# Later chunks of a fused attention and MLP kernel: the denominator ahead of the outer product, small matrix tiles, transfers inside SBUF, a new order

## The chip, the cores and the metric

One Trainium2 chip, one of its cores. A core has a matrix engine (TensorE, PE in the profile, with its weight loads shown as PEld), a vector engine (VectorE, DVE), a scalar engine (ScalarE, ACT), GpSimd (POOL), and SyncE (SP), from whose queue this kernel issues every transfer. SBUF is the working memory of 128 partitions, PSUM the small memory of eight banks that PE writes. The metric is the device time of one launch in microseconds (us); lower is better.

## The reference

```python
# q, k, v: (4 batches, 4 heads, 1088 positions, 32); S1, S2: (8, 32)
def phi(x):                                   # 64 features of each position
    a = einsum('rd,bhsd->bhsr', S1, x)        # 8 numbers
    b = einsum('rd,bhsd->bhsr', S2, x)        # 8 numbers
    return outer(a, b).reshape(..., 64)
kv  = einsum('bhsf,bhsd->bhfd', phi(k), v)    # 64 x 32 for each batch and head
z   = sum(phi(k), over positions)             # 64
num = einsum('bhsf,bhfd->bhsd', phi(q), kv)
den = einsum('bhsf,bhf->bhs', phi(q), z) + 1e-6
x   = (num / den), heads side by side         # 4352 tokens x 128
h   = x @ w_in                                # 128 -> 2048
out = (h * clip(h + 3, 0, 6) / 6) @ w_out     # 2048 -> 128
```

q, k and v are 32-bit floats; S1, S2, w_in and w_out arrive as 64-bit floats and are turned into 32-bit numbers on the chip.

## The kernel before, in words

**Tiling.** The 4352 tokens are cut into nine chunks: chunks 0 to 7 of 512 tokens (two for each batch) and chunk 8 of 256 (the last 64 tokens of every batch). The 2048 hidden columns are cut into eight pairs of 128-column blocks; a *step* is one chunk with one pair, 72 in all. Tokens lie along the free dimension of `x`, so a step takes `x` (128 x 512) and gives `h` (two PSUM banks).

**One step.** PE forms `h` with three matmuls for each block: `x` is kept as a high and a low part (`xh`, `xl`), `w_in` likewise, and `xh*wi_hi + xh*wi_lo + xl*wi_hi` is summed (lines 812, 813, 818). ACT takes relu(h+3) into `g` (826), DVE makes `g = min(g, 6) * h` (829), ACT rounds it into `gh` (833), and POOL or DVE subtracts to get the rest `gl` (837). PE then adds `gh*wo_hi + gh*wo_lo` (858, 859) and `gl*wo_hi` (861) into `o`. These are 12 matmuls of 512 columns for a step, called the MLP matmuls below. After the last pair of a chunk, `o` is scaled and stored.

**Keys and values.** For each batch, nine tiles of 128 positions: PE makes the 16 numbers a, b of every head (`abps_k`, 531), ACT copies them (540), POOL or DVE forms the outer product `ph_k` (559), and PE sums `kvps` over the nine tiles (594), with a column of ones beside `v` so that z comes along. ACT copies the result into `kvb` (619).

**Queries.** Chunks 0 and 1 ("near", `NEAR = 2`) go through `queries`: `abps_q`, `ph_q`, PE transposes into `phps` (714), ACT copies to `phT`, PE multiplies by `kvb` into `nd` (637), which holds numerator and denominator; DVE adds 1e-6, inverts and divides into `x` (644 to 648), and PE transposes `x` into `xps` (665). Chunks 2 to 8 go through `far_queries`: two matmuls make `abps_q` with features along partitions (536), DVE transposes it in 32x32 blocks (544), POOL or DVE forms `ph_q`, DVE transposes again (`pht`, 746), and SP writes it to DRAM (`phd`, four transfers, 752) and reads it back as `phT` (757). After `nd` and the division the same is done for `x`: a DVE transpose (`xt`, 774), four transfers to DRAM (`xd`, 779) and one back (`xT`, 783). ACT and DVE or POOL then split `x` into `xh` and `xl` (682, 686).

**Weights.** Eight loads of 512 columns (`wiraw`, `woraw`); for each, ACT, DVE and POOL put the two 32-bit words together and round into high and low parts (400 to 421).

**Order.** Every engine runs its instructions in program order. That order is decided while the kernel is built: `Plan` collects the operations with an estimated cost, a due time and the buffers they need, and lists them. The due times come from `STEP`, `DUES`, `LEADS` and `SHIFTS`, the order of the first steps from `RAMP`, the first loads from `FIRST_LOADS`. An operation with two engines in its cost may go to either. Buffers are counted in `BUFS`; PSUM has two banks for `a`, four for `h` (two tiles of two), two for `o`.

## Time and profile before

| | |
|---|---|
| runs (us) | 243.3, 243.34, 244.62; median 243.34 |
| profiled execution | 244.0, of which the span from first to last instruction is 242.2 |
| granted PE clock | 1.00 throughout |
| PE busy | 231.9 us, 96% of the span |
| DVE, ACT, POOL busy | 178.0, 168.7, 135.7 us |
| transfers | 23.8 MB in 242 us |

A group row of the profile names the line, engine, operation, output and inputs, then count, total busy time and the mean of one instruction. A matmul's own duration includes its way through the array, and the next one starts before it ends; what counts for PE is the distance from start to start. A matmul of plain 32-bit numbers appears as two records. A row of the timeline gives start, duration and count of a run of like instructions. A row of waits gives the engine and line that waited, what it waited for, and the total, the number of times and the longest.

### The profile page before, as it was taken

To read this page: it belongs to the slowest core of one execution; us is meant where nothing else is said; L and a number is where in the kernel's file an instruction comes from. 1 tells how busy PE (TensorE), PEld (TensorE's weight loads), DVE (VectorE), ACT (ScalarE), POOL (GpSimd) and SP (SyncE) were. 2 spreads that over 40 slices of the span, in tenths; PEclk is the share of its full clock that TensorE was granted. 3 is DMA by queue.
4 is the path that set the end of the run, shared out by engine and by line. 5 is a ranking of instruction groups with operands and counts; after the bars stand their busy time and mean duration, and the time that the engine had idled before them with its cause. 6 is when DMAs were issued, how large, how long until landed. Compare 5 with 4: busy or idle time off the path is not lost.

```text
span 242.2 us, 5410 instructions
## 1 busy us (share of the span) xinstructions
PE 231.9 (96%) x2212; PEld 181.7 (75%) x2212; DVE 178.0 (73%) x223; ACT 168.7 (70%) x213; POOL 135.7 (56%) x88
## 2 busy tenths in 40 slices
PE   8599999998999989999999999999999999999994
PEld 3478777665777757788887888888888888888894
DVE  1597899999987977845675565865867987696771
ACT  3396998764387548678767956778558886777671
POOL 2599899978898704369443575606532130423240
PEclk9999999999999999999999999999999999999999
DMA  6999996666484532400001010000000010000101
GB/s 173 357 408 311 376 352 164 176 164 189 132 211 142 159 93 59 125 3 0 0 1 43 3 43 13 32 0 3 0 13 30 0 46 0 0 0 0 46 0 65
DMA packets 16471, 23.80 MB, mean 98 GB/s; under 512 B 1728, under 2 KB 9024, under 8 KB 16448
## 3 DMA queue, kind: packets, MB, share of 16 engines
q1 hardware_dynamic: 16448, 23.48, 30.0%
q8 instruction: 17, 0.28, 0.5%
q14 instruction: 6, 0.05, 0.1%
HBM read 16.26 MB, written 7.21 MB: 97 GB/s over the span
## 4 chain that ended last, share of the span: by engine, by line
PE 71%; DVE 11%; DMA 6%; ACT 3%; SPq 2%; POOL 2%; issue 2%; DVEq 0%; ACTq 0%
PE o L861 11%; PE h L812 11%; PE o L858 11%; PE o L859 11%; PE h L818 11%; PE h L813 11%; DVE g L829 4%; DMA xd<-xt 3%; DMA kT<-kT_dram 3%; PE nd L637 3%; ACT g L826 2%; DVE pht L746 2%; DVE ph_k L559 2%; SPq L779 1%; DVE ph_q L559 1%
## 5 line engine op out<-in xcount | busy, mean ns | idle before, releaser
L837 POOL TENSOR_TENSOR gl<-g,gh 128x1024 fp32r<-128x1024 f32 (+1 forms) x39 | 90.3, 2323 | 85.7 <-PE o L861 49.8
L829 DVE SCALAR_TENSOR_TENSOR g<-g,h 128x1024 f32<-128x1024 f32 (+1 forms) x72 | 82.5, 1158 | 39.5 <-ACT g L826 38.9
L826 ACT ACTIVATE g<-h 128x1024 f32<-128x1024 f32 (+1 forms) x72 | 69.3, 978 | 28.9 <-PE h L818 28.5
L833 ACT CAST gh<-g 128x1024 fp32r<-128x1024 f32 (+1 forms) x72 | 71.8, 1002 | 21.8 <-PE o L859 8.7
L812 PE MATMUL h<-xh,wi_hi 128*128 128x512 f32 (+1 forms) x148 | 57.2, 387 | 1.5 <-DVE g L829 1.5
L813 PE MATMUL h<-xh,wi_lo 128*128 128x512 f32 (+1 forms) x148 | 55.6, 376 | 0.0
L858 PE MATMUL o<-gh,wo_hi 128*128 128x512 f32 (+1 forms) x144 | 54.8, 383 | 0.0
L818 PE MATMUL h<-xl,wi_hi 128*128 128x512 f32 (+1 forms) x148 | 54.2, 379 | 0.6 <-DVE xl L686 0.6
L859 PE MATMUL o<-gh,wo_lo 128*128 128x512 f32 (+1 forms) x144 | 54.7, 382 | 0.0
L837 DVE TENSOR_TENSOR gl<-g,gh 128x1024 fp32r<-128x1024 f32 (+1 forms) x33 | 42.1, 1287 | 5.3 <-PE o L861 3.3
L861 PE MATMUL o<-gl,wo_hi 128*128 128x512 f32 (+1 forms) x144 | 43.1, 383 | 0.0
L812 PEld LDWEIGHTS h<-xh,wi_hi 128*128 128x128 f32 x148 | 27.7, 187 | 9.6 <-DVE g L829 3.2
L818 PEld LDWEIGHTS h<-xl,wi_hi 128*128 128x128 f32 x148 | 27.6, 188 | 7.1 <-DVE xl L686 1.5
L813 PEld LDWEIGHTS h<-xh,wi_lo 128*128 128x128 f32 x148 | 27.8, 188 | 5.2
L859 PEld LDWEIGHTS o<-gh,wo_lo 128*128 128x128 f32 x144 | 27.0, 188 | 5.7
L858 PEld LDWEIGHTS o<-gh,wo_hi 128*128 128x128 f32 x144 | 27.0, 187 | 5.7
L861 PEld LDWEIGHTS o<-gl,wo_hi 128*128 128x128 f32 x144 | 26.2, 188 | 5.7
L559 POOL TENSOR_TENSOR ph_q<-ab_q 128x512 f32<-128x512 f32 x12 | 13.2, 1105 | 2.8 <-DVE ab_q L544 2.8
L637 PEld LDWEIGHTS nd<-kvb,phT 128*32 128x32 f32 (+1 forms) x480 | 8.8, 113 | 4.2 <-issue 1.9
L637 PE MATMUL nd<-kvb,phT 128*32 128x66 f32 (+1 forms) x480 | 10.9, 223 | 0.7 <-issue 0.3
L594 PEld LDWEIGHTS kvps<-v,ph_k 128*32 128x32 f32 (+3 forms) x504 | 7.2, 113 | 2.7 <-issue 1.8
L559 POOL TENSOR_TENSOR ph_k<-ab_k 128x512 f32<-128x512 f32 (+1 forms) x7 | 7.0, 1012 | 3.5 <-ACT ab_k L540 2.3
(63 smaller groups left out, 164.6 us busy)
## 6 DMA issues: line engine op xcount, KB each, us to landing
phd<-pht SPq DMA_DIRECT2D x24, 128.0 KB, 2.5
phT<-phd SPq DMA_DIRECT2D x6, 512.0 KB, 3.8
qT<-qT_dram SPq DMA_DIRECT2D x8, 256.0 KB, 7.3
wiraw<-w_in_dram SPq DMA_DIRECT2D x4, 512.0 KB, 6.3
woraw<-w_out_dram SPq DMA_DIRECT2D x4, 512.0 KB, 7.8
outT_dram<-os SPq DMA_DIRECT2D x8, 256.0 KB, 2.0
xd<-xt SPq DMA_DIRECT2D x24, 64.0 KB, 2.0
xT<-xd SPq DMA_DIRECT2D x6, 256.0 KB, 2.7
```

Source lines behind the costliest of these rows:

```text
L559: engines[e].tensor_tensor(out, a_, b_, op=ALU.mult)
L637: nc.tensor.matmul(W["nd"][e : e + w, o : o + 2 * DV], T["phT"][:, p, i : i + w], kvb[batch_of(c0 + i)][:, p, :], start=True, stop=True)
L812: nc.tensor.matmul(T["h"][:, u, i:j_], wi_hi[:, f], x, start=True, stop=False)
L813: nc.tensor.matmul(T["h"][:, u, i:j_], wi_lo[:, f], x, start=False, stop=False)
L818: nc.tensor.matmul(T["h"][:, u, i:j_], wi_hi[:, f], x, start=False, stop=True)
L826: nc.scalar.activation(T["g"][:, :, :n], T["h"][:, :, :n], AF.Relu, bias=3.0, scale=1.0)
L829: nc.vector.scalar_tensor_tensor(T["g"][:, :, :n], T["g"][:, :, :n], 6.0, T["h"][:, :, :n], op0=ALU.min, op1=ALU.mult)
L833: nc.scalar.copy(T["gh"][:, :, :n], T["g"][:, :, :n])
L837: engines[e].tensor_tensor(T["gl"][:, :, :n], T["g"][:, :, :n], T["gh"][:, :, :n].bitcast(F32), op=ALU.subtract)
L858: nc.tensor.matmul(o, wo_hi[:, f], T["gh"][:, u, :n], start=first and u == 0, stop=False)
L859: nc.tensor.matmul(o, wo_lo[:, f], T["gh"][:, u, :n], start=False, stop=False)
L861: nc.tensor.matmul(o, wo_hi[:, f], T["gl"][:, u, :n], start=False, stop=last and u == 1)
```

## The change

1. Only chunk 0 is near (`NEAR = 1`). Chunks 1 to 8 take a new `far_queries`.
2. In it the denominator is taken before the outer product: with M = the sum over keys of a times b (8 x 8 for each head), den = b_q . (M^T a_q). A third set of 8 numbers for each query, (M^T S1) q, comes out of the same projection as a and b. POOL multiplies it with b, DVE sums and inverts, POOL divides a by it, and then the outer product is formed; `x` needs no division any more, and no separate numerator and denominator.
3. The projection (line 820 of the new kernel) is eight matmuls of 32 rows by 32 columns of the array for each chunk, the product with kv (868) eight matmuls of 64 by 32, each over 256 tokens. Both results lie in two PSUM banks, with the heads' places in the second bank exchanged. The second product gives `x` already with features along partitions: no transpose, no transfer for `x`.
4. `phT` is moved from SBUF to SBUF by eight transfers of 64 KB (862) in place of a write to DRAM and a read.
5. For every batch kv is accumulated transposed (632), M beside it (643); ACT copies both, PE transposes and multiplies (686, 689), ACT keeps `kvs` and the third set of projection columns (692, 693). Batch 0 does this beside its old `kvps`, which chunk 0 still uses.
6. The rest `gl` (now line 935) goes to POOL alone after the first six steps (`SHARED = 6`); `xl` goes to DVE alone; the outer products of the later chunks go to POOL alone.
7. Every load and store is one contiguous stretch of a DRAM array, which the host lays out.
8. All of the numbers that set the order are new (`RAMP`, `FIRST_LOADS`, `STEP`, `LEADS`, `SHIFTS` and the rest).

```diff
-NEAR = 2
+NEAR = 1
-BUFS = dict(..., x=2, ..., xturn=1, xT=2)
+BUFS = dict(..., x=1, ..., prod=1, kvt=2)
+SHARED = 6
...
+def stretch(t, i, j):
+    return t[i * P : j * P].rearrange("(p x) -> p x", p=P)
...
+        def kvt(_, t, i, T, vbox):
+            ps = place(i)
+            for h in range(H):
+                e = h * Q
+                nc.tensor.matmul(ps[e : e + Q, KVT : KVT + F], vbox[0][:, t, h * DV : h * DV + D],
+                    T["ph"][:, t, h * F : (h + 1) * F], ..., tile_position=(0, e))
+            e = i % 4 * Q
+            nc.tensor.matmul(ps[e : e + Q, KVT + F : KVT + F + Q], a_, b_, ..., tile_position=(0, e))
...
+        def fold(_):
+            nc.tensor.transpose(K["fps"][:, :DM], K["kvt"][:, : 2 * F], ident)
+            for h in range(H):
+                nc.tensor.matmul(K["fps"][e : e + Q, DM : DM + R], s_turn[:, e : e + Q], K["kvt"][:, ...], tile_position=(0, e))
+        def keep(_):
+            nc.scalar.copy(s_proj[:, b, C : C + R], K["fps"][:, DM : DM + R])
+            nc.scalar.copy(kvs[b], K["fps"][:, :DM])
...
-    def far_queries(c, due, psb, ndb, ph_eng):
+    def far_queries(c, due):
+        def proj(_):
+            for (r, b, i, j), h in product(spans, range(H)):
+                e, g = h * Q, (h ^ r) * Q
+                nc.tensor.matmul(T["ps"][r][g : g + Q, ...], s_proj[e : e + Q, b, :], qbox[0][e : e + Q, i:j], ..., tile_position=(e, g))
+        def cp(_, r):
+            nc.vector.transpose(T["ab"][:, r * half : (r + 1) * half], T["ps"][r][:, :half])
+        def prod(_):
+            nc.gpsimd.tensor_tensor(p[:, :, :R], v[:, :, 1, :], v[:, :, 2, :], op=ALU.mult)
+        def invert(_):
+            nc.vector.tensor_reduce(den, parts()[1], axis=mybir.AxisListType.X, op=ALU.add)
+            nc.vector.reciprocal(T["rden"], den)
+        def divide(_):
+            nc.gpsimd.tensor_tensor(v[:, :, 0, :], v[:, :, 0, :], T["rden"].broadcast_to(...), op=ALU.mult)
+        def outer(e, r): ...
+        def turn(_, r):
+            nc.vector.transpose(T["turn"][:, :, r * half : (r + 1) * half]..., src)
+        def move(_):
+            for g, f in product(range(4), range(2)):
+                e = (2 * (g % 2) + f) * Q
+                nc.sync.dma_start(T["phT"][e : e + Q, g // 2, :n], T["turn"][g * Q : (g + 1) * Q, f, :n])
+        def xmm(_):
+            for (r, b, i, j), h in product(spans, range(H)):
+                e, g = (h ^ r) % 2 * HP, h * Q
+                nc.tensor.matmul(T["xps"][r][g : g + Q, ...], kvs[b][e : e + HP, g : g + Q], T["phT"][e : e + HP, h // 2, i:j], ..., tile_position=(e, g))
...
-        o4 = plan.add({POOL: 2.35 * k, DVE: 0.07 + 1.067 * k}, ...)
+        o4 = plan.add({POOL: 2.35 * k, **({DVE: 0.07 + 1.067 * k} if n_step < SHARED else {})}, ...)
```

**Where instructions move: PE ahead of the first MLP matmul.** Names end in the chunk or batch and a buffer's number; `k2` is the first half of batch 1's keys. Before, the last rows ahead of `h_0_0` serve chunks 0 and 1:

```order
L637 MATMUL nd_0_0_369<-kvb0_136,phT_0_357 64x66 x8
L714 MATMUL phps_1_2_384<-ident_131,ph_q1_359 128x128 x4
L714 MATMUL phps_1_0_392<-ident_131,ph_q1_359 128x128 x4
L637 MATMUL nd_0_2_403<-kvb0_136,phT_0_357 64x66 x8
L637 MATMUL nd_1_2_422<-kvb0_136,phT_1_401 64x66 x8
L665 MATMUL xps_0_438<-ident_131,x_0_412 128x128 x2
L637 MATMUL nd_1_0_443<-kvb0_136,phT_1_401 64x66 x8
L665 MATMUL xps_0_438<-ident_131,x_0_412 128x128 x2
L812 MATMUL h_0_0_463<-xh_0_458,wi_hi_156 128x256
```

Now the same place holds chunk 0, batch 0's fold, two tiles of batch 1 and chunk 1's projection:

```order
L713 MATMUL nd_0_2_420<-kvb_133,phT_0_266 64x66 x8
L686 MATMUL kvs_0_447<-ident_128,kvt_0_415 128x128
L689 MATMUL kvs_0_447<-kvt_0_415,s_turn_139 32x8 x4
L740 MATMUL xps_0_455<-ident_128,x_0_431 128x128 x2
L632 MATMUL kvps_1_461<-ph_k2_438,v_2_208 32x64 x4
L643 MATMUL kvps_1_461<-ab_k2_429 32x32
L632 MATMUL kvps_1_461<-ph_k2_438,v_2_208 32x64 x4
L643 MATMUL kvps_1_461<-ab_k2_429 32x32
L740 MATMUL xps_0_455<-ident_128,x_0_431 128x128 x2
L820 MATMUL cps_1_0_484<-qT_1_212,s_proj_137 32x256 x4
L820 MATMUL cps_1_1_485<-qT_1_212,s_proj_137 32x256 x4
L910 MATMUL h_0_0_495<-xh_0_476,wi_hi_154 128x256
```

Chunk 1's transposes and its two `nd` are gone from there; the fold, kv of batch 1 and a projection have come in, and the projection, with the fold and its copies ahead of it, now stands before the first MLP matmul.

**PE in the middle of the program, one far chunk.** Before, chunk 5's product with `kvb`, between MLP matmuls:

```order
L861 MATMUL o_0_0_741<-gl_0_3_1383,wo_hi_158 128x512 x2
L637 MATMUL nd_5_0_1457<-kvb2_140,phT_5_1278 32x66 x16
L637 MATMUL nd_5_2_1476<-kvb2_140,phT_5_1278 32x66 x16
L812 MATMUL h_3_3_1427<-xh_3_1086,wi_hi_156 128x512
L813 MATMUL h_3_3_1427<-xh_3_1086,wi_lo_157 128x512
```

and now:

```order
L916 MATMUL h_4_0_1897<-xl_4_1599,wi_hi_154 128x512
L868 MATMUL xps_5_0_1919<-phT_5_1873,kvs2_142 32x256 x4
L868 MATMUL xps_5_1_1920<-phT_5_1873,kvs2_142 32x256 x4
L956 MATMUL o_2_4_1885<-gh_2_5_1755,wo_hi_156 128x512
L957 MATMUL o_2_4_1885<-gh_2_5_1755,wo_lo_157 128x512
```

Thirty-two matmuls of 66 columns have become eight of 256, and the place stands behind 384 MLP matmuls where it stood behind 133.

**POOL, at the last step of chunk 0.** Before:

```order
L837 TENSOR_TENSOR gl_1_3_1249<-g_1_3_986,gh_1_3_1223 128x1024
L559 TENSOR_TENSOR ph_q7_1290<-ab_q7_1244 128x512 x2
L837 TENSOR_TENSOR gl_1_5_1326<-g_1_5_1201,gh_1_5_1295 128x1024
L415 TENSOR_TENSOR w_wo2_1061<-w_wo2_1061,rest_wo2_1047 128x512
L837 TENSOR_TENSOR gl_0_3_1383<-g_0_3_665,gh_0_3_762 128x1024
```

and now, ahead of `gl_0_7`:

```order
L935 TENSOR_TENSOR gl_1_3_1270<-g_1_3_1157,gh_1_3_1203 128x1024
L935 TENSOR_TENSOR gl_1_7_1287<-g_1_7_1234,gh_1_7_1277 128x1024
L832 TENSOR_TENSOR prods_135<-ab_6_1272 128x16x8
L841 TENSOR_TENSOR ab_4_1174<-ab_4_1174,rden_4_1242 128x16x8
L850 TENSOR_TENSOR ph_4_1345<-ab_4_1174 128x512
L841 TENSOR_TENSOR ab_6_1272<-ab_6_1272,rden_6_1340 128x16x8
L850 TENSOR_TENSOR ph_6_1368<-ab_6_1272 128x512 x2
L832 TENSOR_TENSOR prods_135<-ab_8_1334 128x8x8
L850 TENSOR_TENSOR ph_4_1345<-ab_4_1174 128x512
L935 TENSOR_TENSOR gl_0_7_1410<-g_0_7_1268,gh_0_7_1343 128x1024
```

POOL now carries every `gl` of these steps but one, and small operations of three later chunks stand between two of them.

More of the change, by code (lines that the diff above doesn't have):

```diff
@@ L35 @@
 AB = 2 * H * R
+C = 2 * R
 CH = 512
@@ L271, in order @@
             for op in avail:
-                if op.ready > t or not all(b.held or any(free[g] for g in b.tags) for b in op.bufs):
+                if op.ready > t or not fits(op):
                     continue
@@ L636, in nd @@
                 i = (t + u) * P + e
[L637 removed]
+                nc.tensor.matmul(W["nd"][e : e + w, o : o + 2 * DV], T["phT"][:, p, i : i + w], kvb[:, p, :], start=True, stop=True)
         def norm(_):
@@ new lines, in far_queries @@
+        o1 = plan.add({PE: 0.1 + 0.43 * k}, due - LEAD["ab"], [lq, *done], proj, [qb, *pbs], 2 * n, recs=4 * H * len(spans), small=True)
+        cps = [plan.add({DVE: 0.12 + half / 960}, due - LEAD["cp"] + 0.3 * r, [o1], partial(cp, r=r), [pbs[r], abb]) for r in range(2)]
+        rdb = Buf(("rden",))
+        o2 = plan.add({POOL: 0.4}, due - LEAD["div"], cps, prod, [abb, prodb[0]])
+        o2 = plan.add({DVE: 0.45}, due - LEAD["div"] + 0.1, [o2], invert, [prodb[0], rdb])
+        o2 = plan.add({POOL: 0.4}, due - LEAD["div"] + 0.2, [o2], divide, [abb, rdb])
@@ new lines, in far_queries @@
+        prodb[0] = Buf(("prod",))
+        turned = []
+        for r in range(2):
+            cost = {POOL: 0.12 * blocks + 0.06}
+            o = plan.add(cost, due - LEAD["ph"] + 0.5 * r, [o2], partial(outer, r=r), [abb, phb])
+            turned.append(plan.add({DVE: 0.09 + blocks * F / 960}, due - LEAD["tr"] + 0.5 * r, [o], partial(turn, r=r), [phb, turnb]))
+        o = plan.add({SP: 8 * ISSUE}, due - LEAD["mv"], turned, move, [turnb, phTb], moved=n * 1.024, pieces=8)
+        o = plan.add({PE: 0.1 + 0.43 * k}, due - LEAD["nd"], [o, *done], xmm, [phTb, *xpbs, xhb], 2 * n, recs=4 * H * len(spans), small=True)
@@ L791, in fused_kernel, with step @@
+        split(c, due, [(lambda r=r: T["xps"][r], 0, r * half, (r + 1) * half, [o], xpbs[r]) for r in range(2)], xhb, LEAD)
     o_state = {}
-    def step(i, c, fp):
+    def step(n_step, c, fp):
         c0, n = CHUNKS[c]
-        due = when[i]
+        due = when[n_step]
         T = {}
```

347 lines of the change are left out of this document (192 added, 155 removed).

## The prediction

> **What bounds the kernel now.** I begin with the head of the page and then cut the span at the first MLP matmul and at the end of the interleaved work.
>
> ```profile
> span 242.2 us, 5410 instructions
> ...
> PE 231.9 (96%) x2212; PEld 181.7 (75%) x2212; DVE 178.0 (73%) x223; ACT 168.7 (70%) x213; POOL 135.7 (56%) x88
> ```
>
> ```profile
> 20.40:80.00 59.60, 57.49 (x1132) 42.72 (x1131) 54.98 (x93) 43.00 (x61) 54.74 (x37) 1.00 0.70 216
> 80.00:100.00 20.00, 18.79 (x166) 14.09 (x166) 16.57 (x21) 13.44 (x16) 5.91 (x3) 1.00 0.36 92
> 100.00:239.00 139.00, 138.97 (x644) 113.54 (x644) 94.73 (x87) 100.52 (x112) 61.62 (x28) 1.00 0.05 18
> ```
>
> The columns are the stretch, its length, then busy time and instructions of PE, weight loads, DVE, ACT and POOL, then the granted clock. From the first MLP matmul to 239 PE is idle for 2.1 + 1.2 + 0.0 = 3.3 us, at full clock throughout. The end is set by the amount of work on PE, by when it begins, and little else.
>
> ```profile
> 20.41 0.36 PE L812 MATMUL h<-xh,wi_hi 128*128 128x256 f32 x1
> ...
> 104.12 0.40 PE L812 MATMUL h<-xh,wi_hi 128*128 128x512 f32 x1
> ...
> 113.93 0.40 PE L858 MATMUL o<-gh,wo_hi 128*128 128x512 f32 x1
> ...
> 238.58 0.39 PE L861 MATMUL o<-gl,wo_hi 128*128 128x256 f32 x2
> 239.01 0.38 ACT L877 ACTIVATE os<-o 128x256 f32<-128x256 f32 x1 [2.40 <-PE o L861]
> ```
>
> Between 104.12 and 113.93 stand 42 starts of 512 columns, hence 9.81 / 42 = 0.2333 us each; 256 columns are taken as half, 0.1167.
>
> ```profile
> L858 PE MATMUL o<-gh,wo_hi 128*128 128x512 f32 x128 | 50.7, 396 | 0.0
> L812 PE MATMUL h<-xh,wi_hi 128*128 128x512 f32 x124 | 50.5, 407 | 1.5 <-DVE g L829 1.5
> ...
> L812 PE MATMUL h<-xh,wi_hi 128*128 128x256 f32 x24 | 6.7, 283 | 0.0
> ...
> L858 PE MATMUL o<-gh,wo_hi 128*128 128x256 f32 x16 | 4.1, 278 | 0.0
> ```
>
> Each count stands for three lines of the code, so there are 3 x (128 + 124) = 756 wide and 3 x (24 + 16) = 120 narrow MLP matmuls: 176.4 + 14.0 = **190.4 us**, which the change keeps. The budget of the span is then 20.4 (start) + 190.4 + 3.3 (waits) + 3.4 (last matmul near 238.8 to the end) and, as the rest, 24.7 us of small work on PE. That rest can be checked:
>
> ```profile
> L637 PE MATMUL nd<-kvb,phT 128*32 128x66 f32 x416 | 8.4, 223 | 0.7 <-issue 0.3 <-DVE x L648 0.3
> ...
> L594 PE MATMUL kvps<-v,ph_k 128*32 128x33 f32 x384 | 5.1, 198 | 0.2 <-issue 0.2
> ...
> L531 PE MATMUL abps_k<-s_ab,kT 128*32 128x64 f32 x216 | 4.1, 221 | 0.3 <-DVE w_wi L411 0.3
> L536 PE MATMUL abps_q<-qT,s_sb 128*64 128x256 f32 x24 | 3.7, 400 | 0.0
> ...
> L665 PE MATMUL xps<-ident,x 128*128 128x128 f32 x10 | 2.1, 295 | 0.0
> ...
> L594 PE MATMUL kvps<-v,ph_k 64*32 64x33 f32 x48 | 1.0, 197 | 0.0
> ```
>
> ```profile
> 73.93 1.14 PE L637 MATMUL nd<-kvb,phT 128*32 128x66 f32 x64
> 75.00 0.50 PE L812 MATMUL h<-xh,wi_hi 128*128 128x512 f32 x1
> 75.34 0.39 PE L813 MATMUL h<-xh,wi_lo 128*128 128x512 f32 x1
> ```
>
> After a visit to small work the first MLP matmul takes 75.34 - 75.00 = 0.34, which is 0.11 more than the pace; 17 visits make 1.9. With `nd` 8.4, `kvps` 6.1, keys 3.5 (184 of the 216 records come after 20.4), queries 3.4 (one of the calls comes early, chunk 8's is narrower) and transposes 1.3 (6 of 10), the sum is 24.6. It closes to 0.1.
>
> **The change, term by term: small work on PE.** What goes is `nd`, `abps_q`, the rest of `xps` and `kvps` in its old form: 8.4 + 3.4 + 1.3 + 6.1 = 19.2. What comes is priced from these two rows:
>
> ```profile
> 29.20 0.65 PE L536 MATMUL abps_q<-qT,s_sb 128*64 128x256 f32 x4
> ...
> 45.41 1.08 PE L536 MATMUL abps_q<-qT,s_sb 128*64 128x256 f32 x8
> ```
>
> Two more matmuls (four records), side by side in halves of the array, add 0.43; that is the length of one pass of 256 columns in plain 32-bit numbers. A projection is eight such matmuls on eight different tiles. If all run beside each other it costs 0.43 and the staggered starts of 16 records, at 1.07 / 64 = 0.017 each 0.27: 0.70. Bounds are 0.43 (nothing but the pass) and 8 x 0.43 = 3.4 (one after another). I take 0.70, near the 0.65 of the row of four. In favour of side by side: the `nd` row above ran 32 matmuls of 66 columns in 1.07; alone, each would need 66/256 of 0.43, 0.11, and 32 of them 3.5, so four column tiles did overlap fully. No row shows small tiles that overlap along the rows of the array.
>
> The Trainium skill ("TensorE: Matmul & The Clock Gate", Part 3, measured speedup) gives one pass and about 4 ns for each further tile, checked on sixteen tiles of 32 x 32; by that a product would cost some 0.46, and the forecast, as an estimate from that page, would lie about 3 us lower. The row's 0.65 for four records does not agree with so small a stagger, so I stay with 0.70.
>
> - Projections after the start, chunks 2 to 8: 6 x 0.70 + 0.5 = 4.7.
> - Products with kv, chunks 1 to 8: 7 x 0.70 + 0.5 = 5.4.
> - kv tiles: 36 in all, 11 of them ahead of the first MLP matmul. A tile has ten records (four of 64 columns and one of 32, two records each); at the keys' 4.1 / 216 = 0.019, 25 tiles are 4.75. Bounds: 0.012 as for `kvps` (5.1 / 384 = 0.013), 3.2; or 0.03, if switching tile shapes costs, 7.5.
> - Keys unchanged, 3.5.
> - Folds for three batches: a transpose at 2.1 / 10 = 0.21 and eight records, with ACT's copy between, 0.5 each, 1.5 (0.3 to 0.8 each).
> - Visits: 23 in the new order, 2.5.
>
> The sum is 22.35 against 24.6: **-2.2 us**.
>
> **The start.** Chunk 1's old query path goes from ahead of the first MLP matmul:
>
> ```profile
> 9.33 0.80 PE L531 MATMUL abps_k<-s_ab,kT 128*64 128x64 f32 x20 [2.35 <-DMA kT<-kT_dram]
> ...
> 13.90 0.69 PE L531 MATMUL abps_q<-s_ab,qT 128*64 128x64 f32 x16
> ...
> 17.12 1.09 PE L714 MATMUL phps<-ident,ph_q 128*128 128x128 f32 x8
> ...
> 19.60 0.69 PE L637 MATMUL nd<-kvb,phT 128*64 128x66 f32 x16
> ```
>
> That is 0.65 + 1.0 + 1.2 (two such `nd` rows) = 2.85. In come 11 kv tiles (nine of batch 0, which keeps its old `kvps` too, and two of batch 1), 110 records at 0.016 in a dense run, 1.75, a fold 0.4 and a projection 0.65: 2.8. The wait for the second part of the keys stays, since the same 1.34 MB go ahead of it. So 20.4 stands. From below: if ACT, which no longer copies chunk 1's `phT`, was late there, 19; from above: switches of tile shape and the small copies between, 22.
>
> **The waits.** DVE gives up 27 of its 28 wide `gl` and POOL takes them, and the wait at line 829 below is for DVE behind such work.
>
> ```profile
> PE h L812 <- DVE g L829: 1.5, 2, 1.2
> ```
>
> ```profile
> L837 POOL TENSOR_TENSOR gl<-g,gh 128x1024 fp32r<-128x1024 f32 x36 | 86.4, 2408 | 77.4 <-PE o L861 44.2 <-ACT gh L833 27.1 <-ACT g L826 6.0
> ...
> L837 DVE TENSOR_TENSOR gl<-g,gh 128x1024 fp32r<-128x1024 f32 x28 | 37.9, 1364 | 5.1 <-PE o L861 3.3 <-ACT gh L833 1.6
> ...
> L559 POOL TENSOR_TENSOR ph_q<-ab_q 128x512 f32<-128x512 f32 x12 | 13.2, 1105 | 2.8 <-DVE ab_q L544 2.8
> ...
> L415 POOL TENSOR_TENSOR w_wi<-w_wi,rest_wi 128x512 int32<-128x512 int32 x4 | 5.1, 1281 | 0.0
> L837 POOL TENSOR_TENSOR gl<-g,gh 128x512 fp32r<-128x512 f32 x3 | 3.8, 1292 | 8.3 <-PE o L861 5.7 <-ACT gh L833 2.7
> ...
> L464 POOL TENSOR_TENSOR s_ab<-s_parts 128x64 int32<-128x64 int32 x1 | 0.3, 318 | 1.3 <-DVE s_parts L459 1.3
> ```
>
> DVE falls from 178 to about 138. POOL rises to 63 x 2.41 + 8 x 1.29 + some 22 outer products at 1.1 + 19 of weights + 16 small ones = about 209 of 239. The small ones (`prod`, `divide`, 128 numbers a row) have no row; between 0.1 (the work share of a 512-number row, a quarter of 1.1 being 0.28, less if cheap) and 1.1, I take 0.33, beside the 0.32 of a 64-number row. What matters is the densest part, up to `gl_0_7` in the new order: 14 `gl` (33.7) + 16 outer products (17.6) + 15 weight operations (19.2) + 11 small ones (3.6) = 74.1 us. POOL starts these near 8.8, so it would be through at 82.9 without any wait. PE comes there after 200 MLP matmuls (46.7) and 17.8 of small work from 20.4, at 84.9. The slack is 2 us; POOL waited 59.6 - 54.74 = 4.9 us in that stretch before, with less of its own to do. So a little of it will show on PE: I take waits of 2.5 in place of 3.3, **-0.8**, with bounds 0.5 and 6.
>
> **Transfers.**
>
> ```profile
> phd<-pht SPq DMA_DIRECT2D x24, 128.0 KB, 2.5
> phT<-phd SPq DMA_DIRECT2D x6, 512.0 KB, 3.8
> ...
> xd<-xt SPq DMA_DIRECT2D x24, 64.0 KB, 2.0
> ```
>
> ```profile
> 239.42 0.33 SPq L880 DMA_DIRECT2D outT_dram<-os  x1
> ```
>
> Before, a far chunk waits 2.5 + 3.8 after its last transpose; now eight pieces of 64 KB at 2.0, issued 0.33 to 0.5 apart on SP, about 5 us; the path of `x` (2.0 and more) goes altogether. Between `move` and the product of a chunk stand at least two other steps of PE (5.6 us), the tightest for chunk 1, by hand with 1.7 us to spare. So nothing is booked; without that cover the cost is what lies over, up to 3 us once, which the range holds. Contiguous loads have no visible customer: after the start no wait of PE on a load is left to remove. SP is in order too: a `move` that waits for a turn holds up the stores and weight loads behind it, whose users come several steps later.
>
> **Sum.** 20.4 + 190.4 + 22.4 + 2.5 + 3.4 = 239.1 of span. The profiled execution took 244.0 with 242.2 of span; the median of the runs, 243.34, lies 1.1 above that span, so I add 1.1: **240.2 us**.
>
> **Rivals.**
>
> *The tiles overlap only four at a time* (0.07). Against it speaks nothing measured here; for it, that no row shows row tiles overlapping, and the four column tiles of `nd` are the most that ran at once. Each product then has a second pass of 0.43: 13 full and two half ones after the start 6.0, one in it 0.4: 246.6, slower than before. It decides from the first projection on: 0.70 or 1.13.
>
> *Tiles along the rows that write one bank run one after another* (0.04). Each bank of a projection takes four matmuls from four row tiles, 8 x 0.43 = 3.4 a projection (+2.7); a product with kv has two row tiles, 4 x 0.43 (+1.0). 7.5 x 2.7 + 7.5 x 1.0 = 28: 268. The overlap of the column tiles says nothing on it. The Trainium skill ("TensorEngine Tiling (Array Packing)", Restrictions and Gotchas, Gotcha 1) says that different row tiles cannot access the same PSUM bank at once, and would give this rival; the measured sixteen tiles of its other page speak against a strict reading, and no run here shows either yet.
>
> *POOL becomes the bound up to `gl_0_7`* (0.12). Beyond the 2 us of slack every wait of POOL is one of PE. If POOL waits as it did before, 4.9, and its small operations cost 0.5, PE waits 2.9 + 1.9 more: 245. For it: the 74.1 against 76.1. Against: operations stand in the order in which they come due, and 33 `gl` no longer compete for DVE.
>
> *The start does not hold* (0.12): switches between the 32-column and 128-column shapes and the copies of the fold in ACT's queue put the first MLP matmul at 22: 242.
>
> *Better than the sum* (0.10): start at 19, waits 0.5, small work at the lower bounds: 236.8.
>
> **How the numbers follow.** The forecast case has 0.55, with 238.2 to 242.2 of its own (0.5 for the kv tiles, 1 for the waits, 1 for the start). A measurement of this kernel can tell about 1% from no change, so faster means below 240.9 and slower above 245.8. Faster: 0.37 of the forecast and 0.10 of the better case, 0.47. Same: 0.18 of the forecast, 0.12 of the start, 0.07 of POOL, 0.37. Slower: 0.05 of POOL, 0.11 of the tiles, 0.16. The range runs from 236.5 to 246.6; the serial tiles and the ends of the other cases are left out.
>
> **What would show it.** Right: a projection and a product near 0.70 from start to next MLP matmul; first MLP matmul at 20 to 21; the kv tiles 0.19 each; PE idle after it below 3 us; POOL near 209 busy, DVE near 138; span near 239. Wrong: products of 1.1 or 1.7 to 3.4 (tiles); waits of PE on `gl` in the stretch to 85 (POOL); waits on `phT` (transfers); a first MLP matmul beyond 22.

## The result and the profile after

The changed kernel takes 247.27 us (median of 245.63, 246.08, 248.46 and 248.53) against 243.39 for the kernel before: ratio 1.0116 with an interval of 1.0069 to 1.0162, so slower by about 1.2%. Forecast were 240.2 and a range of 236.5 to 246.6. Further runs of the same kernel on another chip gave 247.25 (ratio 1.0114, 1.0068 to 1.0160). Here and below, times are medians of all runs and ratios leave out runs in the slower state, among them one of 319.6 us at a granted clock of 0.66 (the variant with the arrays as before).

The head of the page after, then the same cuts of the span as before (length; busy time and instructions of PE, weight loads, DVE, ACT, POOL; granted clock; share of the DMA engines; GB/s):

```profile
span 243.8 us, 4939 instructions
...
PE 232.0 (95%) x1958; PEld 176.6 (72%) x1959; DVE 132.6 (54%) x184; ACT 169.4 (69%) x228; POOL 210.2 (86%) x136
```

```profile
20.40:80.00 59.60, 57.29 (x783) 41.86 (x783) 46.47 (x73) 45.93 (x70) 56.84 (x41) 1.00 0.32 96
80.00:100.00 20.00, 18.32 (x129) 12.44 (x128) 12.73 (x24) 10.09 (x14) 17.79 (x16) 1.00 0.36 92
100.00:239.00 139.00, 138.17 (x701) 110.41 (x699) 63.14 (x67) 100.75 (x116) 122.06 (x60) 1.00 0.07 22
```

POOL's 210 and DVE's 133 are as forecast (209, 138), and the transfers of the stretch to 80 us fell to less than half (0.70 to 0.32). PE's idle time did not fall: 1.7 us in the middle stretch where there were 1.2, 0.8 in the last where there was none. The timeline gives the two ends:

```profile
22.09 0.39 PE L910 MATMUL h<-xh,wi_hi 128*128 128x256 f32 x1
...
239.50 0.50 PE L959 MATMUL o<-gl,wo_hi 128*128 128x256 f32 x2 [0.25 <-POOL gl L935]
240.03 0.38 ACT L975 ACTIVATE os<-o 128x256 f32<-128x256 f32 x1 [2.63 <-PE o L959]
```

The first MLP matmul comes 1.7 us later than before, the end of PE 1.0 later. PE's waits name the places (line, what was waited for, then total, number of times and longest):

```profile
PE o L956 <- ACT gh L931: 1.7, 1, 1.7
PE cps L820 <- issue: 1.4, 1, 1.4
PE abps_k L571 <- issue: 1.3, 1, 1.3
PE o L956 <- ACT kvt L682: 1.2, 1, 1.2
...
PE xps L868 <- DMA phT<-turn: 0.7, 1, 0.7
```

"Issue" is time in which an engine waits for nothing that the profile shows. Both cases lie ahead of the first MLP matmul and, as the timeline shows, in the middle of a run of like matmuls whose data were there already: after 4 of 32 records of the keys of batch 1, and after 13 of 16 of chunk 1's projection.

```profile
13.79 0.31 PE L571 MATMUL abps_k<-s_all,kT 128*32 128x64 f32 x4
15.40 0.58 PE L571 MATMUL abps_k<-s_all,kT 128*32 128x64 f32 x26 [1.31 <-issue]
...
19.52 0.65 PE L820 MATMUL cps<-qT,s_proj 32*32 32x256 f32 x13
21.54 0.62 PE L820 MATMUL cps<-qT,s_proj 32*32 32x256 f32 x3 [1.37 <-issue]
```

The row of `phT` shows less than was lost. A product with kv mostly takes 0.59 us from its start to the next MLP matmul. Two took longer (chunk 7's near 118, chunk 5's near 137), because the eight pieces of `phT` land one after another and each group of its matmuls waits for its own piece:

```profile
117.19 1.09 PE L868 MATMUL xps<-phT,kvs 64*32 64x256 f32 x6
118.99 0.64 PE L868 MATMUL xps<-phT,kvs 64*32 64x256 f32 x10 [0.70 <-DMA phT<-turn]
119.56 0.73 PE L959 MATMUL o<-gl,wo_hi 128*128 128x512 f32 x2
...
137.01 1.40 PE L868 MATMUL xps<-phT,kvs 64*32 64x256 f32 x16
138.35 0.50 PE L956 MATMUL o<-gh,wo_hi 128*128 128x512 f32 x1
```

The last pieces landed at 118.85 and 137.64. The two products took 2.37 and 1.34 us, together 2.5 more than twice 0.59, and the row counts 0.7 of that.

The budget of the span, with small work counted from start to start:

| us | forecast | measured |
|---|---|---|
| first MLP matmul | 20.4 | 22.1 |
| MLP matmuls | 190.4 | 190.4 |
| small work and visits | 22.4 | 23.6 |
| waits of PE after the start | 2.5 | 3.9 |
| last matmul to the end | 3.4 | 3.8 |
| span | 239.1 | 243.8 |

Of the 23.6, 1.8 is that uncounted part of the wait for `phT`. With it on the other side, small work is 21.8 and the waits are 5.7.

### The profile page after: what moved, and what is told of

It reads as the page before. It is cut to its first block, busy times and chain, and to the rows that moved or that the text cites. A ratio compares the mean times of both kernels' runs of the same rounds, so it can differ in the third digit from the quotient of the medians.

```text
span 243.8 us, 4939 instructions
## 1 busy us (share of the span) xinstructions
PE 232.0 (95%) x1958; PEld 176.6 (72%) x1959; DVE 132.6 (54%) x184; ACT 169.4 (69%) x228; POOL 210.2 (86%) x136
## 3 DMA queue, kind: packets, MB, share of 16 engines
q1 hardware_dynamic: 9264, 17.46, 22.1%
## 4 chain that ended last, share of the span: by engine, by line
PE 77%; POOL 11%; DMA 3%; issue 3%; SPq 3%; ACT 1%; POOLq 1%; DVE 1%
PE h L910 12%; PE o L959 12%; PE o L956 11%; PE h L911 11%; PE o L957 11%; PE h L916 11%; POOL gl L935 6%; POOL ph L850 3%; PE kvps L632 2%; DMA kT<-kT_dram 2%; SPq L862 2%; PE abps_k L571 2%; PE xps L868 1%; PE cps L820 1%; PE kvps L617 1%
## 5 line engine op out<-in xcount | busy, mean ns | idle before, releaser
L935 POOL TENSOR_TENSOR gl<-g,gh 128x1024 fp32r<-128x1024 f32 (+1 forms) x71 | 161.5, 2297 | 19.7 <-ACT gh L931 10.0
L931 ACT CAST gh<-g 128x1024 fp32r<-128x1024 f32 (+1 forms) x72 | 72.3, 1005 | 23.6 <-DVE g L927 8.6
L959 PE MATMUL o<-gl,wo_hi 128*128 128x512 f32 (+1 forms) x144 | 44.0, 387 | 0.2 <-POOL gl L935 0.2
L850 POOL TENSOR_TENSOR ph<-ab 128x512 f32<-128x512 f32 (+1 forms) x16 | 16.0, 1016 | 0.6
L856 DVE STREAM_TRANSPOSE turn<-ph 128x512 f32<-128x512 f32 (+1 forms) x16 | 10.2, 659 | 1.1 <-POOL ph L850 1.1
L760 DVE TENSOR_TENSOR xl<-xps,xh 128x256 fp32r<-128x256 f32 (+1 forms) x18 | 6.6, 401 | 5.4 <-ACT xh L756 4.5
L756 ACT CAST xh<-xps 128x256 fp32r<-128x256 f32 (+1 forms) x18 | 5.7, 366 | 5.3 <-PE xps L868 4.0
L825 DVE STREAM_TRANSPOSE ab<-cps 128x256 f32<-128x256 f32 (+1 forms) x16 | 6.5, 415 | 4.9 <-PE cps L820 4.5
L584 DVE TENSOR_TENSOR ph_k<-abps_k,ab_k 128x512 f32<-128x512 f32 (+1 forms) x15 | 8.4, 610 | 0.0
```

Source lines behind the costliest of these rows:

```text
L850: engines[e].tensor_tensor(out, a_, b_, op=ALU.mult)
L856: nc.vector.transpose(T["turn"][:, :, r * half : (r + 1) * half].rearrange("p f (t w) -> p t f w", w=Q), src)
L931: nc.scalar.copy(T["gh"][:, :, :n], T["g"][:, :, :n])
L935: engines[e].tensor_tensor(T["gl"][:, :, :n], T["g"][:, :, :n], T["gh"][:, :, :n].bitcast(F32), op=ALU.subtract)
L959: nc.tensor.matmul(o, wo_hi[:, f], T["gl"][:, u, :n], start=False, stop=last and u == 1)
```

## The experiments

The theory after the result: **PE's instructions arrive too late.** The page has this row for the transfers that carry instructions:

```profile
q8 instruction: 15, 0.25, 0.5%
```

That is 16.4 KB each, and PE's 1958 + 1959 instructions make 15.3 blocks of 256. Each record of a matmul has its weight load beside it, so a block is about 126 records, and the idle times of 1.31, 1.37 and 1.17 (the row that names `kvt`) stand right ahead of records 220, 346 and 599, one and two blocks apart. With all of PE's instructions in the trace counted, 449, 705 and 1217 come before them: 256 and 512 apart. ACT, which the third row names, had ended `kvt` at 32.14, 0.9 us before PE went on. The trace's instruction transfers, in us:

```
block boundary (record)     PE there   transfer begins, lands   PE goes on
changed, 220                10.0       12.86   13.88            15.40
changed, 346                15.4       19.12   20.17            21.54
changed, 599                28.3       30.72   31.67            33.05
before,  219                11.8       15.27   16.30            17.72 (no stall)
```

("PE there" is PE at the boundary before, when the block can be asked for.) A block takes 4.7 to 6.1 us from there until PE can use it: 2.4 to 3.7 before its transfer begins (the share of the DMA engines was 1.04, 1.03 and 0.69 in these stretches of the changed kernel), 1.0 to move, 1.4 to 1.5 more. PE used up the blocks ahead of the three stalls in 3.6 to 4.8 us; 126 MLP matmuls take 126 x 0.2333 = 29. The rivals: a data wait that the profile cannot name, or simply more work ahead of the first MLP matmul.

**The changed kernel again.**

> The changed kernel without an edit, to see which of its numbers come back. Its four runs fell into two pairs, 245.6 and 246.1 us at a mean granted clock of 0.997, and 248.5 twice at 0.986. Theory clock: the upper pair is the same schedule with about 5 us of half clock somewhere (1.1% of 240 us is 2.6 us, the distance of the pairs); then every run near 248.5 shows 0.985 to 0.987, and a profile of one shows a stretch of lower clock ahead of the last 4 us. Theory schedule: the upper pair has other waits of PE; then a profile near 248.5 shows them at full clock. Both expect the two idle times marked issue on PE near 14 and near 20, of 1.3 us each, the one of 1.7 before line 956 near 86, and the first MLP matmul at 22.1.

245.91 at a mean granted clock of 0.998, then 247.26, 247.63 and 247.24 at 0.991, 1.000 and 0.991. The idle times near 20 and 86 returned (1.46, 1.81). The one near 14 returned with the same length, but four records earlier and with another reason:

```profile
15.56 0.82 PE L571 MATMUL abps_k<-s_all,kT 128*32 128x64 f32 x30 [1.37 <-DMA kT<-kT_dram]
```

Here the load of batch 1's first keys landed at 15.43, where it landed at 13.65 in the first profile. The instruction block landed at 14.23; with the 1.4 to 1.5 from above it could be used near 15.7. So at this place PE goes on at the later of two arrivals, and taking away the instruction stall alone would have gained next to nothing in this execution. In the variants below these keys landed between 13.4 and 16.1. The idle time of 1.17 near 32 was 0.31 here, all of it ACT's, which ended `kvt` at 32.53.

The level of the time is not only clock: the run at 1.000 took 247.6. No run near 248.5 came back, so the two theories on the pairs stay open. But stretches at half clock do occur, as the next runs show.

**Warm-up matmuls cut into eight.**

```diff
-        nc.tensor.matmul(warm, ones[:, :P], ones, start=True, stop=True)
+        for i in range(8): nc.tensor.matmul(warm[:HP, : CH // 8], ones[:, :HP], ones[:, : CH // 8], start=True, stop=True)
```

> Each of the thirteen warm-up matmuls of 512 columns is cut into eight of 64, so that PE's program has some 182 more instructions ahead of its real work and hardly more to do. Theory instruction fetch: PE's program comes in blocks of 256 instructions (126 records of the profile), a block is asked for when the one before it is begun and takes 5 to 6 us while the loads run; the idle times stand at the records 220, 346 and 599, multiples of that block apart. Then they leave their old instructions (the fifth record of the keys of batch 1, the fourteenth of chunk 1's projection), stand some 91 records earlier in the program, where the block before them took longer to run, and sum to 0.5 us or so instead of 2.7 ahead of the first MLP matmul, which comes at 19.5 to 20.5; time 1.5 to 2.5 us below that of the changed kernel. Theory data: the idle times are waits for data that the profile does not name; then they stay at the same instructions with the same length, the first MLP matmul at 22, the time within 0.5 us.

```profile
15.48 0.28 PE L632 MATMUL kvps<-ph_k,v 128*32 128x64 f32 x2
17.42 0.40 PE L632 MATMUL kvps<-ph_k,v 128*32 128x64 f32 x10 [1.67 <-issue]
```

The keys of batch 1 (after 0.63 of waiting for their load) and the projection now run through; the stall sits two records into a kv tile, at record 349 of a program with 99 more records (2057 against 1958). 706 instructions come before it, as 705 came before one of the stalls in the changed kernel: the same block boundary. So it is the place in the program that stalls, not the data: theory instruction fetch on the place, wrong on the gain. The sum of the stalls fell only from 2.7 to 1.7, and the first MLP matmul came at 22.5. The clock shows part of why: PE ran at half clock from 17.6 to 21.0 (`nd`, 1.16 us in the changed kernel, took 2.03) and again from 89.3 to 92.7, each time behind an idle time (1.67, 1.80). Time 247.08 (1.0112; 1.0065 to 1.0158), as the changed kernel.

**Fewer instructions, with some work left out.**

```diff
         def kvt(_, t, i, T, vbox):
+            if b == 0 and i >= 4: return
```

> Batch 0's transposed kv and M are summed over its first four tiles only (the other five, 50 records of PE, are left out; nothing else changes), so PE's program has 100 instructions less ahead of the first MLP matmul, and some 0.9 us less to do there. Theory instruction fetch: the boundaries of the 256-instruction blocks, at records 220 and 346, now fall 50 records of the old numbering later: into nd, just when the block is in (15.4), and into the first steps' matmuls, where one block lasts long. Both stalls of 1.3 go: first MLP matmul at 19 to 20.3 against 22.1 to 22.5, a gain of more than 2 where the work left out is 0.9. Rival, work alone: 0.9, at 21.3 to 21.6, and stalls of 1.3 us stay somewhere ahead of it. How much of the gain reaches the end is open: the moved-back instructions of the earlier run gave theirs back within 6 us.

```profile
14.46 0.27 PE L713 MATMUL nd<-kvb,phT 128*64 128x66 f32 x1
15.50 1.15 PE L713 MATMUL nd<-kvb,phT 128*64 128x66 f32 x31 [0.77 <-issue]
...
19.69 0.39 PE L910 MATMUL h<-xh,wi_hi 128*128 128x256 f32 x1
```

242.04 us, ratio 0.9945 (0.9916 to 0.9974) to the kernel before, and the clock at 0.997 to 1.000 in all ten runs. The boundary falls into `nd` as expected, one stall of 0.77 is left, the first MLP matmul comes 2.8 us earlier than in the repeat of the changed kernel (2.4 than in its first profile) and the last one 3.2 earlier, for an estimated 0.9 of work. Work alone is refuted. What holds PE next is the load of batch 1's keys (0.41) and POOL's outer product of them (0.73), so the fetch was not the only thing in the way of an earlier start. Part of the gain in time is the clock: no run here was below 0.997.

**Fewer instructions, the same work.**

```diff
-                for e in range(0, P, w):
+                for e in range(0, P, HP):      # and HP for w in the matmul
```

> The keys of batches 1 to 3 use two column tiles of 64 in place of four of 32, as batch 0 does: the same products, 126 records (252 instructions, one block) fewer in all, 18 of them ahead of the first MLP matmul. Theory instruction fetch: the stall near 20 moves behind the projection, and the later ones near 32 to 46 (0.2 to 1.2 us) go or move; time 0.5 to 1.5 us below the changed kernel. Rival, work alone: a tile of 128 positions costs 0.126 us either way by the rows of batch 0 (0.031 a record) and of the later ones (0.016), so nothing changes within 0.3 us.

246.05 us, ratio 1.0077 (1.0048 to 1.0107): 1.2 below the changed kernel's median, though the two intervals overlap, so the gain is not clear of noise. The trace has 216 instructions less (4723 against 4939). The stall near 20 and the ones from 32 to 46 are gone, the one near 14 stayed (1.26). In the profiled run, at 0.985, two half-clock stretches (16.1 to 19.5, 87.8 to 91.2) took most of it back. The run at 1.000 took 245.1, the one at 0.999 took 246.1.

**The same instructions later.**

```diff
-    for op in plan.order():
+    for op in delayed(plan.order(), {"keys_k2": "nd_0_2", "proj_1": "h_0_0_1_1"}):   # moved behind the named operation, with what depends on it
```

> The changed kernel with two groups of PE instructions moved back: the first keys of batch 1 (32 records) from ahead of nd of chunk 0 to behind it, chunk 1's projection (16 records) from ahead of the first step's matmuls to behind them. What depends on them moves too where it has to; the work is the same. Theory instruction fetch: the block boundary at record 220 then falls into nd, which waits for kvb until about 14.4 anyway, and the next one, at record 346, into the first MLP matmuls, of which one block lasts over 20 us. The stalls of 1.3 and 1.4 go, the first MLP matmul comes at 19 to 20, and the time is 2 to 3 us below that of the changed kernel. Rival, amount of work: only the 0.6 us of the projection leaves the stretch ahead of the first MLP matmul; it comes at 21.5, and the time falls by 0.6 at most, or not at all where chunk 1 becomes late.

246.73 (1.0107; 1.0069 to 1.0145). The first MLP matmul came 1.5 us earlier than in the repeat (20.95 against 22.48), but at 28 us the kernel was 1.1 behind the repeat, and from 36 us on 1.4 to 1.8. The fetch stall did shrink, to 0.71 near 15 with none marked issue after it, but other engines took the gain. The projection, now behind the first MLP matmul, waited for a transpose of DVE:

```profile
24.67 0.63 PE L820 MATMUL cps<-qT,s_proj 32*32 32x256 f32 x8 [0.57 <-DVE ab L825]
```

With this wait the projection's visit took 1.77 us (23.46 to 25.23), and waits for POOL's `ph_k` (0.79) and ACT's `xh` (0.46) stand ahead of the first MLP matmul. Both theories missed: the gain at the start is real, and worth nothing.

**Two `gl` to DVE, then `gl_0_7` alone.**

```diff
-            engines[e].tensor_tensor(T["gl"][:, :, :n], ...)
+            engines[DVE if (c, fp) in ((1, 3), (1, 7)) else e].tensor_tensor(T["gl"][:, :, :n], ...)   # then: (c, fp) == (0, 7)
```

> Two subtractions gl (chunk 1, pairs 3 and 7) that stand on POOL shortly ahead of gl_0_7 go to DVE, at the same place of the order. Theory POOL: the idle 1.7 us of PE near 86, which the waits put down to ACT at line 931, comes from POOL, which runs from 68 to 86 without a gap; with 4.8 us less there it goes, and the time falls by 1.7 us. Theory ACT: gh is late by itself (ACT or DVE behind other work); then the wait stays at 1.7, or grows by up to 1 us since DVE has 2.4 us more, and the time stays or rises.

> gl_0_7 alone goes from POOL to DVE, at its place in the order. With two earlier subtractions off POOL (the run before) POOL waited 4.7 us for the transposes of chunk 6's projection and began gl_0_7 only 0.16 us earlier; so the theory is now: not POOL's load but its order, gl_0_7 behind the small operations of chunks 4, 6 and 8, each of which waits for DVE. Then gl_0_7 on DVE ends near 85 instead of 86.3, the buffer for the next gh is free by then, and the idle 1.7 us of PE near 86 falls to 0.5 or less: time 1 to 1.5 us lower at equal clock. Rival: the wait is ACT's own; it stays at 1.7.

POOL's timeline of the changed kernel ahead of PE's idle time (85.77 to 87.46):

```profile
73.43 4.78 POOL L935 TENSOR_TENSOR gl<-g,gh 128x1024 fp32r<-128x1024 f32 x2
...
80.58 2.10 POOL L850 TENSOR_TENSOR ph<-ab 128x512 f32<-128x512 f32 x2
...
83.94 2.39 POOL L935 TENSOR_TENSOR gl<-g,gh 128x1024 fp32r<-128x1024 f32 x1
```

and ACT's, which waits for the buffer that this last one, `gl_0_7`, frees:

```profile
86.36 1.04 ACT L931 CAST gh<-g 128x1024 fp32r<-128x1024 f32 x1 [2.47 <-POOL gl L935]
```

With two `gl` on DVE POOL had 4.8 us less, but waited 4.71 for transposes that DVE now did later, and began `gl_0_7` at 83.78 instead of 83.94:

```profile
78.01 0.46 POOL L832 TENSOR_TENSOR prods<-ab 128x128 f32<-128x128 f32 x1 [4.71 <-DVE ab L825]
```

PE's wait fell from 1.69 to 0.61, but PE went on at 87.30 instead of 87.46: it had only come later, with a new wait of 0.52 at 75 among the reasons. The time was 246.48 (1.0103; 1.0028 to 1.0178), 0.8 below the changed kernel on the same chip and not clear of it, so neither theory holds as a whole. With `gl_0_7` alone on DVE the wait was 0.55, about as expected, but 1.7 us of new waits for `phT` stood at 105 (0.66 and 1.03): chunk 8, whose transposes stand behind that operation on DVE, was late. Instead of 1 to 1.5 us less the time was 248.85 (1.0157; 1.0116 to 1.0198). The profiled execution, 248.89, holds two windows at half clock as well:

```profile
17.80:21.20 3.40, 2.18 (x46) 1.12 (x45) 2.76 (x8) 2.16 (x7) 3.40 (x5) 1.00 1.04 397
21.20:24.60 3.40, 2.83 (x11) 2.02 (x12) 2.35 (x5) 1.66 (x3) 2.39 (x3) 0.50 1.02 373
24.60:28.00 3.40, 3.40 (x12) 2.55 (x10) 0.93 (x4) 1.02 (x1) 1.72 (x2) 0.50 0.17 60
```

The clock column reads 0.50 for 6.8 us, behind a window with two idle times in it; at 30 us this run is 2.6 us behind the repeat of the changed kernel. The prediction had no term for that.

**The heads' places not exchanged.**

```diff
-                e, g = h * Q, (h ^ r) * Q
+                e, g = h * Q, h * Q
...
-                e, g = (h ^ r) % 2 * HP, h * Q
+                e, g = h % 2 * HP, h * Q
```

> The heads keep their places in the second PSUM bank, in the projection and in the product with kv (both without the exclusive or), so that the second half of the tokens uses the same tiles of the array as the first. Theory tiles side by side: all eight small matmuls overlap in the changed kernel (0.59 us from their start to the next MLP matmul); now two share each tile and take turns, one pass of 0.43 more for each of 14 products after the start and one in it: 1.0 us a product, time 6 us above that of the changed kernel. Theory one bank at a time: eight matmuls already take turns somewhere, and 0.59 is not one pass; then a product stays within 0.1 us of 0.59 and the time within 1.5 us.

The same projection in the changed kernel and here, in two timelines:

```profile
47.39 0.66 PE L820 MATMUL cps<-qT,s_proj 32*32 32x256 f32 x16
47.98 0.50 PE L910 MATMUL h<-xh,wi_hi 128*128 128x512 f32 x1
```

```profile
47.54 1.06 PE L820 MATMUL cps<-qT,s_proj 32*32 32x256 f32 x16
48.54 0.50 PE L910 MATMUL h<-xh,wi_hi 128*128 128x512 f32 x1
```

0.59 became 1.00, about the one pass of 0.43 more: all eight tiles do run side by side in the changed kernel. Over all products that is 5.1 us of PE; waits of PE after the start fell from 3.4 in the repeat to 1.5 beside it. The span rose by 3.1 and the time by 1.9, from 247.25 to 249.13 (1.0203; 1.0154 to 1.0251), a half and a third of the 6 expected. A longer PE hid the other engines' lateness.

**The arrays as before.**

```diff
-    return t[i * P : j * P].rearrange("(p x) -> p x", p=P)
+    return t[:, i:j]                         # and the host's arrays whole
```

> The DRAM arrays lie as before the change (rows of the whole array, a load takes a piece of every row), everything else as changed. Theory early keys: the contiguous loads are what brought the first keys sooner (PE's 2.3 us of waiting for kT in the kernel before is gone in the changed one); undone, PE waits 1.5 to 2.5 us again between 6 and 10, and since the instruction fetch stalls come later in the program, part of it is absorbed there: first MLP matmul at 22.5 to 24, time 0.5 to 2 us higher. Rival: the first loads' new order did that; the first MLP matmul stays at 22.1 to 22.5 and the time within 0.5.

247.55 (1.0107; 1.0060 to 1.0154). PE did not wait for the first keys (0.32 us near 7.4), and the first MLP matmul came at 22.4, as with contiguous arrays. So the rival's numbers came, and the contiguous loads brought nothing that these runs can tell. That the new order of the first loads did it is not shown: the kernel before, profiled again at the end of this section, has no such wait either.

**Through DRAM again.**

```diff
-                nc.sync.dma_start(T["phT"][e : e + Q, g // 2, :n], T["turn"][g * Q : (g + 1) * Q, f, :n])      # eight
+            nc.sync.dma_start(d[...], T["turn"][g * Q : (g + 1) * Q, :, :n])                                   # four
+            nc.sync.dma_start(T["phT"][:, :, :n], d)
```

> phT of the later chunks goes through DRAM again, in four writes of 128 KB and one read, in place of eight transfers of 64 KB inside SBUF. By rows: a chunk's move takes 5.2 us of issues and 2.0 us of landing in the changed kernel (at 111.6 to 118.9), the way through DRAM 2.0 of issues, 2.5 and 3.8 of landings, 8.5 in all. Theory hidden: only the chunk whose product already waits 0.7 us near 118 waits longer, by about 1.3 us; time 0.5 to 2 us higher. Rival, the transfers are what carries the change: every chunk from 1 on waits, and the time is more than 4 us higher. Rival, the eight issues cost more than they save: the wait near 118 goes and the time falls by up to 0.7.

```profile
PE xps L868 <- DMA phT<-phd: 4.4, 3, 2.6
```

250.47 (1.0225; 1.0183 to 1.0267). Three chunks wait, 4.4 us in all, where two chunks lost 2.5 in the changed kernel, and two windows at half clock stand at the longest (119.0 to 125.8). Moving `phT` inside SBUF instead of through DRAM is worth about 3 us in this order (250.47 against 247.27), part of it clock. The transfers were neither hidden nor late for every chunk, and the time lies between what those two theories gave.

**Removing the waits.** First the 64-column keys with two `gl` on DVE; then two edits more; then the 50 records of batch 0 moved behind the first step:

```diff
-            engines[e].tensor_tensor(T["gl"][:, :, :n], ...)
+            engines[DVE if (c, fp) in ((1, 6), (3, 6)) else e].tensor_tensor(T["gl"][:, :, :n], ...)
# then (2, 4) as well, and in delayed(): {"outer_4_1": "gate_3_6"}; then {"kvt_0_4": "h_0_0_1_1"} as well
```

> The keys as in the run before this one, and gl of chunk 1, pair 6, and of chunk 3, pair 6, on DVE instead of POOL, at places where DVE waits. By the traces: the second is right ahead of chunk 7's division and outer products, whose phT comes 0.7 us late near 118; the first makes room of 2.4 us on POOL ahead of gl_0_7, of which some 0.8 are useful (the next gl waits for its gh). Sum 1.5 us, with the keys 2 to 3 below the changed kernel, level with the kernel before. Rival, the waits only move: less than 0.7 us below the changed kernel, new idle times of PE elsewhere.

> The kernel of the 64-column keys with gl of (chunk 1, pair 6) and (3, 6) on DVE, and two edits more: gl of (2, 4) on DVE too (it stands on POOL between the halves of chunk 5's outer product, whose phT came 0.7 us late near 135), and the second half of chunk 4's outer product, with its transpose, moved behind gl_0_7 (PE waited 0.9 us near 85 for what gl_0_7 frees). Theory: both waits go and nothing new is late, 1.6 us below the run before, 242.8, which is 0.5% below the kernel before. Rival: POOL and DVE are both tight there and the wait returns at another place, within 0.5 us of 244.4.

> The same with the last five tiles of batch 0's transposed kv, its fold and chunk 1's projection moved from ahead of the first MLP matmul to behind the first step: nothing is left out. Theory instruction fetch: with these 75 records later, the first MLP matmul comes at 18 to 19; but the blocks that hold them arrive every 5 to 6 us while the loads run (until about 28), so what PE has to get through by then is the same, and of the 1.5 to 2 us gained at the start no more than 0.7 reaches the end. Rival, the first MLP matmul sets the end: the whole gain reaches it, 241 us.

The first: 244.41, ratio 1.0034 (1.0001 to 1.0067) to the kernel before; 2.8 below the changed kernel's median, 0.8% by the ratios. The waits are 0.91 near 85, 0.29 near 116 and 0.71 near 135. With the keys alone they were 1.80, 0.28 and 0.72, so the two `gl` brought 0.9 near 85 and moved nothing at the other two places. The second: 244.32, 1.0010 (0.9984 to 1.0036), the wait near 85 at 0.44, the one near 135 unchanged; the rival held, and nothing was gained over the first. The third: 250.59 (1.0265; 1.0216 to 1.0315), PE idle for 2.2 us from 16.8 on, waiting for POOL's outer product of batch 1's keys, half clock from 19.3 to 26.2, the first MLP matmul at 20.55 in spite of the 75 records that went from ahead of it. Theory and rival both missed. No version that does the whole work beat the kernel before.

**The kernel before, again.**

> The kernel before, unedited, for a second profile of it. Theory: its parts come back as in its first profile, first MLP matmul at 20.4, idle of PE after it 3.3 us, 3.2 us from the last matmul to the end, no half-clock stretch ahead of the last 2 us. The changed kernel and its variants show 3.7 to 4.0 at the end, with the arrays laid out either way; if this one shows them too, the 0.6 us that the end seemed to lose is scatter between executions and not the change.

243.8 us; first MLP matmul at 19.5, idle after it 3.6, 3.2 us from the last matmul to the end. The wait of 2.35 for the second part of the keys, from which the prediction took its start of 20.4, is gone here (0.72 instead, for DVE), with nothing changed: starts of this kernel scatter by 0.9 at least, and against this profile the changed kernel starts 2.6 later. The last store landed in 1.7 us in both profiles of this kernel, in 1.7 in three variants of the changed kernel (the same instructions later, some work left out, the third under "Removing the waits") and in 2.3 to 2.7 in the rest, so the 0.6 us at the end may be scatter; these runs do not settle it.

## Why the prediction was wrong

**The start: 1.7 us, not 0.** The sum of work ahead of the first MLP matmul was right within what the rows show, and one wait was better than booked: the second part of the keys could start at 7.6 instead of 9.3 (8.4 in the second profile of the kernel before). The step "So 20.4 stands" failed because I summed PE time and never asked whether PE's instructions would be there. Nine kv tiles of batch 0 and two of batch 1 are 110 records of 0.016, a dense instruction stream put where the loads fill the DMA engines: 1.31 + 1.37 of stalls, then 1.17 at 32, of which ACT alone would have cost 0.3. In the repeat the load of batch 1's keys was as late as the first of these blocks. The rival "the start does not hold" named 22, which came, but by luck: it meant switches of tile shape and ACT's copies, and no wait of PE ahead of the first MLP matmul names either. The row "issue" of the kernel before (0.2 to 0.3 each) was the same thing in small; I had passed over it. The Trainium skill ("Runtime: NRT & Kernel Launch", Instruction fetch mechanics) says that instructions come in blocks of 16 KiB, 256 of them, one fetched while the other runs, and that the cost is mostly hidden. Block and size agree with the trace; hidden it is only while a block lasts longer than the 4.7 to 6.1 us measured here.

**Small work: -1.3, not -2.2.** It went from 24.9 (with 3.2 at the end) to 23.6. The parts that came were priced high, if anything (forecasts in brackets): projections 3.95 (4.7), kv tiles 4.35 (4.75), folds 1.0 (1.5). The products took 6.35 (5.4), but 1.8 of that is the wait for `phT` shown above; without it they took 4.5. The parts that went were taken at busy times, which overlap: from start to start `nd` was 7.8 (8.4), `kvps` 5.3 (6.1), `abps_q` 3.2 (3.4) and `xps` 0.8 (1.3), 17.1 in place of 19.2. Both should have been counted from start to start. Without the wait the change in small work would have been -3.1.

**Waits: 5.7, not 2.5.** The largest part is a term that the prediction put at nothing. "So nothing is booked" for the transfers compared 5.6 us of cover with eight issues 0.33 to 0.5 apart and a landing of 2.0. For chunk 7 the issues came 0.74 apart on average, 5.2 us from first to last (111.65 to 116.86), and the last piece landed at 118.85, 7.2 us after the first issue; PE came to the product after 5.5. With chunk 5 this cost 2.5 us. The rival of POOL up to `gl_0_7` named the next place: 1.69 comes from exactly that subtraction. The estimate there compared POOL's load with PE's progress; the order weighs more, since POOL with two `gl` less began `gl_0_7` as late. The fetch stall of 1.17 makes up most of the rest.

**From span to time.** I added 1.1 to a span, the profiled execution had 1.8, and the median lies 1.6 above that one. The upper pair of times has a mean clock of 0.985 to 0.986. The five profiles taken at 0.985 or 0.986 (warm-up cut into eight, 64-column keys, `gl_0_7` on DVE, through DRAM, the third under "Removing the waits") each show two windows of half clock, 3.41 us each, and the one at 0.992 (arrays as before) shows one. The changed kernel's own 248.5 runs have no profile, so for them this is inferred, and the 247.6 at full clock in the repeat has no explanation. The Trainium skill ("TensorE: Matmul & The Clock Gate", Part 1, What's actually happening) has the clock follow PE's activity in free-running windows of 3413 ns, between half and full. The traces agree: the half-clock stretches are 3.41 us or twice that, and with the warm-up cut into eight the stretches between changes of clock last 13.65, 3.41, 68.27, 3.41 and 153.6 us, all multiples of 3.413. They stand at or behind PE idle times of 1.3 to 2.6 us. Such an idle time is not enough: those of 1.3 to 1.8 in both profiles of the changed kernel were followed by none, and what decides is not shown here.

**What was right.** Eight small matmuls on eight tiles run side by side at 0.59 (0.70 forecast), so both rivals on the tiles fall, also the one by the Trainium skill ("TensorEngine Tiling (Array Packing)", Restrictions and Gotchas, Gotcha 1): four row tiles that write one bank did overlap. POOL's and DVE's loads were right to 1 and 5 us, and the 0.11 of a visit holds (a product to the second MLP matmul behind it: 48.32 - 47.39 = 0.93).

## What to carry to other kernels

Count PE's instructions as well as its time: where small matmuls come 60 to the us while loads are running, the next block of 256 instructions can be what is late, and "issue" in the middle of a run of like matmuls is its mark. Moving such work later did not pay in either run that tried (246.73 and 250.59): loads and other engines held PE instead. Fewer instructions brought the first MLP matmul forward, with the same work too: from 22.1 to 21.2 with the 64-column keys, and to 20.2 with the same keys where the start ran at full clock. A transfer in pieces is as late as its last piece: add the issues on one queue to the landing, and look for the wait inside a run of matmuls too, where no row of waits may show it. And a wait of PE of 1.5 us can cost twice, once itself and once by 3.4 us at half clock (1.6 us near 90 with the warm-up cut into eight), in some executions and not in others.
